# Scores of the second batch: two products a head instead of three, with the keys' high and low parts stacked in the rows

## The chip, the cores and the metric

The kernel runs on one core of a Trainium2 chip. The core has five engines that work at the same time and wait for each other by semaphores: TensorE (PE, matrix products, with its weight loads PEld), VectorE (DVE), ScalarE (ACT), GpSimd (POOL) and SyncE (SP, which issues most of the transfers). The metric is the device time of one execution in microseconds. The time of the kernel before is the median of three runs.

## What is computed

Three layers follow each other. The first is attention over 2 batches of 8 heads, 768 positions, 64 values per head, in which a position sees the 96 positions up to itself and the first 8 of the sequence, with a linear bias by distance:

```
scores = (q @ k.T) / sqrt(64) + bias;  scores = where(keep, scores, -1e9)
a = softmax(scores);  attn = a @ v
```

The second layer normalises each of the 1536 tokens by its root mean square and applies a gated MLP (512 to 1536 and back): `(silu(xn @ w_gate) * (xn @ w_val)) @ w_out`. The third routes each token to two of eight experts by noisy logits and adds the two experts' outputs by their weights.

## The kernel before

The positions are cut into 12 tiles of 128 queries: tiles 0 to 5 are the first batch, 6 to 11 the second. A tile `ti` runs through `prep` (PE transposes its keys and queries into PSUM, other engines copy them out), `scores` (for four pairs of heads: products into one PSUM bank per pair, then on DVE, line 428, bias and minimum, on ACT, line 431, the exponential), `turn` (PE transposes the probabilities, line 444), `values` (products with v, lines 489 and 493) and `rms` and `norm` (normalisation, a small power on POOL in line 574, transposition to xT). The columns of a score product are a window: the tile's own 128 keys and behind them the tile before, whose first 32 places hold the sequence's first keys; tile 6, the first of its batch, has 128 columns, tiles 7 to 11 have 256. `same` copies the keys of the tile before into the window on POOL (line 394).

The score of a product of 64 values fills 64 of PE's 128 rows. Tiles 1 to 11 use all 128: the rows of the key tile `kT` hold an even head in rows 0 to 63 and the odd head beside it in rows 64 to 127, and the query tiles `q..e` and `q..o` hold the even or the odd head in its rows and zeros in the others. `qtile` makes these tiles; the zeros are written once per buffer, on POOL (line 341).

Tiles 6 to 11 (`ti >= F32T`) work with a split of each fp32 number into a high part in the fp32r format and a low part, the difference. `kT[0]` holds the keys' high parts and `kT[1]` their low parts, `q0..` the queries' high and `q1..` their low parts. ACT writes the high parts (line 385), DVE the low ones (line 389 for keys, 391 for queries). A head's scores are the sum of three products (lines 422 to 424): high by high, low by high, high by low.

The stage of tiles 3 to 11 is interleaved with the first chunk of the MLP, so far as tokens are ready. A visit (0, t0, 2) takes two token tiles through four hidden blocks: `up` (line 689, products pz), `hidden` (lines 697 to 703, the last step dl on POOL), `down` (line 716, products acc). Meanwhile `conv` takes apart the MLP's weights (lines 629 to 643, on ACT, POOL and DVE). The kernel is written as a program order with a few forced successions (`follow`); from slot 12 on, a scheduler that simulates the engines' times arranges each engine's instructions. An edit in one place therefore moves instructions around it too. After the last slot the attention's memory is closed and given to the pool `late`, in which further weights of the MLP are put.

Of the kernel before, what the change touches and what calls it, by code (L numbers as in the profile page):

```python
# [9 lines left out]
F32 = mybir.dt.float32  # L10
# [9 lines left out]
P = 128  # L20
# [85 lines left out]
def fused(ctx: ExitStack, tc: tile.TileContext, q, k, v, n_global, n_local, w_gate, w_val, w_out,  # L106
          rms_g, w_router, w_noise, noise, w1, w2, out):
    nc = tc.nc
    w_gate, w_val, w_out = (w.bitcast(I32) for w in (w_gate, w_val, w_out))
    B, H, S, D = q.shape  # L110
# [28 lines left out]
    F32T = NB  # L139
# [145 lines left out]
    qz = {}  # L285
# [44 lines left out]
    def qtile(x, m, ti):  # L330

        key = x, m, ti // NB
        if key not in qz:
            one = m == "e"
            full = ti < F32T
            qz[key] = t = at.tile([P, NP, P], F32 if full else F32R, name=f"q{x}{m}{ti}", tag=f"q{x}{m[0]}", bufs=1 if one else 2)
            r = slice(D, P) if one else slice(0, D)
            if full:
                zero = nc.gpsimd.memset(t[r], 0.0)
            else:  # L340
                zero = nc.gpsimd.tensor_scalar(t[r], ident[r].rearrange("p (o d) -> p o d", o=1).broadcast_to([D, NP, P]),
                                               0.0, None, op0=ALU.mult)
            follow(zero.ins, state["pool"])
        return qz[key]

    def prep(ti, wide, hook=None):
# [5 lines left out]
        qn, kn = state.pop(("in", ti))  # L352
        full = ti < F32T
# [8 lines left out]
        else:  # L362
            qb = [[qtile(x, m, ti) for m in ("e", f"o{ti % 2}")] for x in range(1 if full else 2)]
            qT = {(x, h): qb[x][h % 2][:, h // 2, :] for x in range(len(qb)) for h in range(H)}
            qd = [(slice(m * D, (m + 1) * D), qb[0][m], qb[-1][m]) for m in range(2)]
        operands = ((kn, [(slice(0, P), kT[0][:, :, P:], kT[1][:, :, P:])], 1.0), (qn, qd, -(D ** -0.5)))
        p3s = {}
        state["cur", ti] = (W, C0, nblk, kT, qT)
        for step, (cs, src, dst, sc) in enumerate([(slice(0, NP),) + o for o in operands] if ti else
# [11 lines left out]
            for n, (rs, dh, dl) in enumerate(dst):  # L381
                if wide and n:
                    nc.vector.tensor_scalar(dh[rs, cs], p3[rs, cs], sc, None, op0=ALU.mult)
                else:
                    nc.scalar.activation(dh[rs, cs], p3[rs, cs], AF.Copy, scale=sc)
                if full:
                    continue
                if sc == 1.0:
                    nc.vector.tensor_sub(dl, p3, dh.bitcast(F32))
                else:  # L390
                    nc.vector.scalar_tensor_tensor(dl[rs], p3[rs], sc, dh[rs].bitcast(F32), op0=ALU.mult, op1=ALU.subtract)

        def same(dst, src):
# [14 lines left out]
    def scores(u, wide):  # L408
# [9 lines left out]
        for t in range(2):  # L418
            h = pair(ti, pr)[t]
            sl = slice((h % 2) * D, (h % 2 + 1) * D) if ti < HALF else slice(0, P)  # L420
            o = psc[:, t * W:(t + 1) * W]
            prods = ((0, 0), (1, 0), (0, 1)) if ti >= F32T else ((0, 0),)
            for n, (a, c) in enumerate(prods):
                seq(nc.tensor.matmul(o, qT[a, h], kT[c][sl, h // 2, C0:], start=(n == 0), stop=(n == len(prods) - 1)))  # L424
        for t in range(2):
# [652 lines left out]
    n = 0  # L1078
# [212 lines left out]
```

## Time and profile before

| | |
|---|---|
| median of 3 runs | 792.91 us (789.46 to 793.13) |
| profiled execution | 795.31 us, its span 793.6 us |
| mean granted TensorE clock | 0.992 of full |
| busy: PE, DVE, ACT, POOL | 97%, 59%, 45%, 38% of the span |
| instructions on PE | 5044 products, 5044 weight loads |
| scores of the second batch on PE | 91.6 to 197.3 us |

The profile is one execution, and times in it are counted from the span's start. The durations of PE's products overlap, since they are pipelined; what a product takes from the others is read from the distance of the starts. A view by line groups instructions of one line and shape; a view by stretch gives the busy time between two moments; the timeline shows single instructions, with equal neighbours merged, and in brackets how long the engine stood idle before one and who ended that.

### The profile page before, as it was taken

The page shows a single profiled execution, that of the slowest core. Times are in us where ns is not written, and L with a number is a line of the kernel's source. Part 1 is how long each engine was busy: PE and PEld are TensorE (multiplying, and loading weights), DVE is VectorE, ACT ScalarE, POOL GpSimd, SP SyncE. Part 2 cuts the span into 40 slices and gives each one's busy share as a digit, 9 for nine tenths or more (in the row PEclk, how much of TensorE's full clock was granted, in tenths as well). Part 3 has the DMA queues.
Part 4 walks back from the last instruction along what each step waited for, and adds up shares of the span by engine and source line. Part 5 has one row for each costly group of instructions (what it writes and reads, how often), then busy time and mean ns, then how long its engine had stood idle before and what let it go on. Part 6 is the DMA issues. An engine that isn't in the chain of part 4 may idle for free.

```text
span 793.6 us, 13818 instructions
## 1 busy us (share of the span) xinstructions
PE 768.9 (97%) x5044; PEld 693.6 (87%) x5044; DVE 467.0 (59%) x1073; ACT 358.9 (45%) x800; POOL 305.0 (38%) x343
## 2 busy tenths in 40 slices
PE   8999999999999999999999999799999999999993
PEld 5898999999788888889999889688999999999993
DVE  4898887666477887334445577533545454545542
ACT  5776767665444444113332455433333434344440
POOL 3247852241375566001422244531424343434311
PEclk9999999999999999999999999999999999999997
DMA  8464432260233340010116419953544738282011
GB/s 188 101 182 122 117 97 55 54 173 2 80 120 93 108 132 1 1 53 1 28 27 154 140 32 241 321 172 112 172 146 156 212 113 252 71 258 76 34 41 36
DMA packets 116840, 88.78 MB, mean 112 GB/s; under 512 B 49449, under 2 KB 100649, under 8 KB 116768
## 3 DMA queue, kind: packets, MB, share of 16 engines
q1 hardware_dynamic: 107920, 65.43, 29.9%
q0 software_dynamic: 7120, 19.27, 7.3%
q10 hardware_dynamic: 1728, 3.15, 1.4%
q8 instruction: 42, 0.69, 0.4%
q14 instruction: 30, 0.25, 0.1%
HBM read 75.18 MB, written 13.34 MB: 112 GB/s over the span
## 4 chain that ended last, share of the span: by engine, by line
PE 79%; DVE 7%; issue 5%; ACT 3%; DMA 3%; POOL 1%; POOLq 0%; ACTq 0%; SPq 0%; DVEq 0%
PE pz L983 15%; PE pz L689 13%; PE ac L1023 12%; PE acc L716 12%; PE pv L689 5%; PE pg L689 5%; PE ac L1000 4%; PE ps L424 3%; PE po L493 2%; PE pp L444 2%; PE pg L950 1%; PE lg L785 1%; PE pb L1055 1%; DVE s L428 1%; PE pt L380 1%
## 5 line engine op out<-in xcount | busy, mean ns | idle before, releaser
L983 PE MATMUL pz<-gh,sa 128*128 128x256 f32 (+7 forms) x576 | 155.9, 338 | 0.0
L983 PEld LDWEIGHTS pz<-gh,sa 128*128 128x128 f32 x576 | 103.4, 188 | 4.6
L983 PE MATMUL pz<-gl,sa 128*128 128x256 f32 (+7 forms) x288 | 97.0, 337 | 0.0
L716 PE MATMUL acc<-wo,dh 128*128 128x512 f32 x288 | 88.5, 400 | 1.0 <-ACT dh L702 1.0
L1023 PE MATMUL ac<-zh,sb 128*128 128x480 f32 (+4 forms) x320 | 86.2, 363 | 0.0
L990 ACT ACTIVATE zh<-pz 128x256 fp32r<-128x256 f32 (+7 forms) x72 | 35.1, 488 | 107.8 <-PE pz L983 105.5
L991 DVE SCALAR_TENSOR_TENSOR zl<-pz,zh 128x256 fp32r<-128x256 f32 (+7 forms) x72 | 39.8, 553 | 71.8 <-ACT zh L990 71.5
L689 PE MATMUL pz<-xTh,wg 128*128 128x256 f32 x352 | 75.0, 290 | 1.3 <-ACT xTh L593 1.0
L689 PE MATMUL pz<-xTh,wv 128*128 128x256 f32 x352 | 74.2, 288 | 0.0
L671 ACT ACTIVATE sa<-wab 128x512 fp32r<-128x512 f32 x72 | 45.3, 630 | 56.6 <-PE ac L1023 39.7
L689 PEld LDWEIGHTS pz<-xTh,wg 128*128 128x128 f32 x352 | 58.8, 191 | 3.5 <-ACT xTh L593 1.2
L703 POOL TENSOR_TENSOR dl<-u,dh 128x256 fp32r<-128x256 f32 (+1 forms) x38 | 38.4, 1010 | 60.9 <-ACT dh L702 44.2
L1023 PEld LDWEIGHTS ac<-zh,sb 128*128 128x128 f32 x320 | 58.0, 188 | 3.3
L675 DVE TENSOR_TENSOR sa<-wab,sa 128x512 fp32r<-128x512 f32 x51 | 36.3, 713 | 41.6 <-ACT sa L671 41.3
L716 PEld LDWEIGHTS acc<-wo,dh 128*128 128x128 f32 x288 | 51.1, 188 | 9.9 <-ACT dh L702 1.6
L689 PEld LDWEIGHTS pz<-xTh,wv 128*128 128x128 f32 x352 | 58.1, 190 | 0.4
L431 ACT ACTIVATE p<-s,mx 128x256 f32<-128x256 f32 (+1 forms) x96 | 46.2, 483 | 23.2 <-DVE mx L428 21.8
L893 POOL DMA_INDIRECT metad<-meta,si x24 | 23.8, 991 | 84.6 <-DVE si L865 78.5
L983 PEld LDWEIGHTS pz<-gl,sa 128*128 128x128 f32 x288 | 54.1, 188 | 2.3
L940 POOL DMA_INDIRECT xg<-x2d,ic x30 | 29.8, 994 | 67.1 <-PE pg L950 60.1
L1023 PE MATMUL ac<-zl,sb 128*128 128x480 f32 (+4 forms) x160 | 53.0, 357 | 0.0
L675 DVE TENSOR_TENSOR sb<-wab,sb 128x512 fp32r<-128x512 f32 x67 | 47.2, 704 | 9.5 <-ACT sb L671 8.7
(249 smaller groups left out, 1870.7 us busy)
## 6 DMA issues: line engine op xcount, KB each, us to landing
wab<-in_moe_w_dram SPq DMA_DIRECT2D x128, 256.0 KB, 5.0
rg<-in_moe_w_gate_dram SPq DMA_DIRECT2D x12, 512.0 KB, 3.8
rv<-in_moe_w_val_dram SPq DMA_DIRECT2D x12, 512.0 KB, 3.9
ro<-in_moe_w_out_dram SPq DMA_DIRECT2D x12, 512.0 KB, 3.7
vn<-in_v_dram SPq DMA_DIRECT2D x12, 256.0 KB, 4.6
out_dram<-zero SPq DMA_DIRECT2D x1, 3072.0 KB, 13.9
x2d<-x ACTq DMA_DIRECT2D x12, 256.0 KB, 5.9
kn<-in_k_dram SPq DMA_DIRECT2D x11, 256.0 KB, 3.0
```

Of the source, the lines that this page charges most:

```text
L431: state["e"] = nc.scalar.activation(p[:, :W], s[:, :W], AF.Exp, scale=-1.0, bias=mx[:, h:h + 1], accum_out=sm[:, h:h + 1]).ins
L671: cp = nc.scalar.activation(wp[:, 0], src, AF.Copy)
L675: (nc.gpsimd if pool else nc.vector).tensor_sub(wp[:, 1], src, wp[:, 0].bitcast(F32))
L689: mm = nc.tensor.matmul(pz, a[:, cs], x[:, tt:tt + nt, c, :], start=(n == 0), stop=(n == 3 * DC - 1))
L703: (nc.gpsimd if ci < len(CHUNKS) - 1 else nc.vector).tensor_sub(dl, u, dh.bitcast(F32))
L716: nc.tensor.matmul(acc[t], a[:, tt], w, start=(f == CHUNKS[ci][0] and n == 0), stop=(end and n == 2))
L940: self.last = nc.gpsimd.indirect_dma_start(out=xg[:m], out_offset=None, in_=x2d[:self.rows], in_offset=bass.IndirectOffsetOnAxis(ap=self.i ...
L983: mm = nc.tensor.matmul(pz[:, :cap], a[:, cs], x[:, c, :cap], start=(k == 0), stop=(k == 3 * DC - 1))
L990: nc.scalar.activation(dh[:, :cap], pz[:, :cap], AF.Relu)
L991: nc.vector.scalar_tensor_tensor(dl[:, :cap], pz[:, :cap], 0.0, dh[:, :cap].bitcast(F32), op0=ALU.max, op1=ALU.subtract)
L1000: mm = nc.tensor.matmul(o, a[:, s * P:s * P + m], w[:, cuts(s)[x]], start=(f == 0 and k == 0), stop=(f == FB2 - 1 and k == 2)).ins
L1023: nc.tensor.matmul(acc[c][:, :cap], w[:, c * P:(c + 1) * P], a[:, :cap], start=(f == 0 and k == 0), stop=(f == FB2 - 1 and k == 2))
```

## The change

For tiles 6 to 11 the split parts lie differently. `kT[0]` now belongs to the even heads and `kT[1]` to the odd ones: an even head's high part in rows 0 to 63 and its low part in rows 64 to 127, an odd head's high part in rows 64 to 127 and its low part in rows 0 to 63. The query's high tile `q0..` holds the high part in both halves, by a copy of 64 rows on DVE, where it had zeros; `q1..` holds the low part in the rows of the keys' high part and zeros as before. A head's scores are then two products: `q0` by `kT` gives high by high and high by low in one sum over 128 rows, and `q1` by `kT` gives low by high. For each tile ACT writes the keys' high part in two instructions of 64 rows, DVE subtracts in two instructions of 64 rows that write the other half of the rows, and DVE makes the two copies of the queries' high parts. The zero filling of the three `q0` buffers is gone.

```diff
--- before.py
+++ after.py
@@ -337,6 +337,8 @@
             r = slice(D, P) if one else slice(0, D)
             if full:
                 zero = nc.gpsimd.memset(t[r], 0.0)
+            elif x == 0:
+                return qz[key]
             else:
                 zero = nc.gpsimd.tensor_scalar(t[r], ident[r].rearrange("p (o d) -> p o d", o=1).broadcast_to([D, NP, P]),
                                                0.0, None, op0=ALU.mult)
@@ -363,7 +365,11 @@
             qb = [[qtile(x, m, ti) for m in ("e", f"o{ti % 2}")] for x in range(1 if full else 2)]
             qT = {(x, h): qb[x][h % 2][:, h // 2, :] for x in range(len(qb)) for h in range(H)}
             qd = [(slice(m * D, (m + 1) * D), qb[0][m], qb[-1][m]) for m in range(2)]
-        operands = ((kn, [(slice(0, P), kT[0][:, :, P:], kT[1][:, :, P:])], 1.0), (qn, qd, -(D ** -0.5)))
+        both = [slice(m * D, (m + 1) * D) for m in range(2)]
+        kd = [(both[m], kT[m][:, :, P:], kT[m][:, :, P:]) for m in range(2)]
+        if full:
+            kd = [(slice(0, P), kT[0][:, :, P:], None)]
+        operands = ((kn, kd, 1.0), (qn, qd, -(D ** -0.5)))
         p3s = {}
         state["cur", ti] = (W, C0, nblk, kT, qT)
         for step, (cs, src, dst, sc) in enumerate([(slice(0, NP),) + o for o in operands] if ti else
@@ -386,8 +392,9 @@
                 if full:
                     continue
                 if sc == 1.0:
-                    nc.vector.tensor_sub(dl, p3, dh.bitcast(F32))
+                    nc.vector.tensor_sub(dl[both[1 - n]], p3[rs], dh[rs].bitcast(F32))
                 else:
+                    nc.vector.tensor_copy(dh[both[1 - n]], dh[rs].bitcast(F32))
                     nc.vector.scalar_tensor_tensor(dl[rs], p3[rs], sc, dh[rs].bitcast(F32), op0=ALU.mult, op1=ALU.subtract)
 
         def same(dst, src):
@@ -419,7 +426,7 @@
             h = pair(ti, pr)[t]
             sl = slice((h % 2) * D, (h % 2 + 1) * D) if ti < HALF else slice(0, P)
             o = psc[:, t * W:(t + 1) * W]
-            prods = ((0, 0), (1, 0), (0, 1)) if ti >= F32T else ((0, 0),)
+            prods = ((0, h % 2), (1, h % 2)) if ti >= F32T else ((0, 0),)
             for n, (a, c) in enumerate(prods):
                 seq(nc.tensor.matmul(o, qT[a, h], kT[c][sl, h // 2, C0:], start=(n == 0), stop=(n == len(prods) - 1)))
         for t in range(2):
```

The order of the instructions, engine by engine, in the two built kernels (the numbers behind the names tell tiles and buffers apart; `ps7_0` are the scores of tile 7, first pair; the lines of the changed kernel lie 2 to 7 higher):

PE, the first pair of tile 7 (`kT7` keys, `q0e` and `q1e` the queries' high and low parts), the first head's products and then the second's, before:

```order
L424 MATMUL ps7_0_1510<-kT7_0_1279,q0e6_1070 128x256
L424 MATMUL ps7_0_1510<-kT7_0_1279,q1e6_1074 128x256
L424 MATMUL ps7_0_1510<-kT7_1_1280,q0e6_1070 128x256
L424 MATMUL ps7_0_1510<-kT7_0_1279,q0e6_1070 128x256
L424 MATMUL ps7_0_1510<-kT7_0_1279,q1e6_1074 128x256
L424 MATMUL ps7_0_1510<-kT7_1_1280,q0e6_1070 128x256
```

and now:

```order
L431 MATMUL ps7_0_1507<-kT7_0_1277,q0e6_1070 128x256
L431 MATMUL ps7_0_1507<-kT7_0_1277,q1e6_1072 128x256
L431 MATMUL ps7_0_1507<-kT7_0_1277,q0e6_1070 128x256
L431 MATMUL ps7_0_1507<-kT7_0_1277,q1e6_1072 128x256
```

The two products with `kT7_1`, the third of each head, are gone.

DVE, the preparation of tile 8 (`kT8` keys, `q0e`, `q1e`, `q0o`, `q1o` queries; line 428 the scores' reduction for tile 7, line 501 the output of tile 6), before:

```order
L389 TENSOR_TENSOR kT8_1_1579<-pt8_1580,kT8_0_1578 128x4x128
L501 TENSOR_TENSOR x6_1613<-po6_1370,rs6_1610 128x512
L391 SCALAR_TENSOR_TENSOR q1e6_1074<-pt8_1587,q0e6_1070 64x512
L428 ISA s7_1_1651,mx7_1508<-nbias_74,ps7_2_1644 128x256
L428 ISA mx7_1508 128x1
L428 ISA s7_3_1655,mx7_1508<-nbias_74,ps7_2_1644 128x256
L428 ISA mx7_1508 128x1
L572 TENSOR_SCALAR ss6_1616<-ss6_1616 128x1
L391 SCALAR_TENSOR_TENSOR q1o06_1076<-pt8_1587,q0o06_1072 64x512
```

and now (the lines 428, 501, 389 and 391 are 435, 508, 395 and 398; `CAST` is the copy):

```order
L508 TENSOR_TENSOR x6_1610<-po6_1369,rs6_1607 128x512
L395 TENSOR_TENSOR kT8_0_1571<-pt8_1573,kT8_0_1571 64x4x128
L435 ISA s7_1_1646,mx7_1505<-nbias_74,ps7_2_1641 128x256
L435 ISA mx7_1505 128x1
L397 CAST q0e6_1070<-q0e6_1070 64x512
L398 SCALAR_TENSOR_TENSOR q1e6_1072<-pt8_1582,q0e6_1070 64x512
L435 ISA s7_3_1650,mx7_1505<-nbias_74,ps7_2_1641 128x256
L435 ISA mx7_1505 128x1
L579 TENSOR_SCALAR ss6_1613<-ss6_1613 128x1
L395 TENSOR_TENSOR kT8_1_1572<-pt8_1573,kT8_1_1572 64x4x128
L397 CAST q0o06_1071<-q0o06_1071 64x512
L398 SCALAR_TENSOR_TENSOR q1o06_1074<-pt8_1582,q0o06_1071 64x512
```

Three instructions stood there for tile 8, and now six, with the same reductions between them.

PE, around the end of the value products of tile 11 (`po11`); `pz8_3` are the MLP's products of the last hidden block of the visit before the last in this chunk, `acc0_8` its down products. Before:

```order
L493 MATMUL po11_2865<-rn11_2327,ph11_3_2974 128x64
L689 MATMUL pz8_3_3293<-xTh2_2305,wg3_990 128x256 x2
L689 MATMUL pz8_3_3293<-xTl2_2306,wg3_990 128x256
L689 MATMUL pz8_3_3293<-xTh2_2305,wg3_990 128x256 x2
L689 MATMUL pz8_3_3293<-xTl2_2306,wg3_990 128x256
L689 MATMUL pz8_3_3293<-xTh2_2305,wg3_990 128x256
L689 MATMUL pz8_3_3293<-xTh2_2305,wv3_1159 128x256
L689 MATMUL pz8_3_3293<-xTl2_2306,wv3_1159 128x256
```

and now:

```order
L500 MATMUL po11_2840<-rn11_2314,ph11_3_2947 128x64
L696 MATMUL pz8_3_3266<-xTl2_2293,wv3_1161 128x256
L696 MATMUL pz8_3_3266<-xTh2_2292,wv3_1161 128x256 x2
L696 MATMUL pz8_3_3266<-xTl2_2293,wv3_1161 128x256
L696 MATMUL pz8_3_3266<-xTh2_2292,wv3_1161 128x256 x2
L696 MATMUL pz8_3_3266<-xTl2_2293,wv3_1161 128x256
L696 MATMUL pz8_3_3266<-xTh2_2292,wv3_1161 128x256
L723 MATMUL acc0_8_3197<-wo2_721,dh8_2_3245 128x512 x2
```

Behind the last value product stood 19 products of `pz8_3`, and now 8; the others are ahead of it. Then the same 12 down products follow in both.

## Rows read from the trace of the kernel before

**Rows 1.** the page's part 1: busy time, share of the span, instructions

```profile
PE 768.9 (97%) x5044; PEld 693.6 (87%) x5044; DVE 467.0 (59%) x1073; ACT 358.9 (45%) x800; POOL 305.0 (38%) x343
```

**Rows 2.** by stretch: us, busy PE, PEld, DVE, ACT, POOL; clock, DMA share, GB/s

```profile
84.00:112.00 28.00, 27.36 (x238) 25.78 (x237) 25.61 (x68) 18.57 (x55) 21.28 (x25) 1.00 0.50 134
112.00:127.00 15.00, 15.00 (x134) 13.70 (x133) 10.38 (x28) 9.63 (x26) 3.69 (x7) 1.00 0.23 59
...
176.00:207.00 31.00, 31.00 (x348) 28.91 (x346) 17.41 (x50) 16.48 (x46) 6.30 (x8) 1.00 0.01 2
207.00:216.00 9.00, 7.10 (x51) 5.39 (x48) 3.13 (x6) 5.06 (x11) 5.29 (x7) 1.00 0.53 175
```

**Rows 3.** waits of PE over the span: us in total, times, longest

```profile
PE ps L424 <- DVE mx L428: 1.1, 2, 0.6
...
PE pz L689 <- ACT xTh L593: 1.0, 1, 1.0
```

**Rows 4.** timeline of all engines around the end of the attention

```profile
206.67 0.73 POOL L703 TENSOR_TENSOR dl<-u,dh 128x256 fp32r<-128x256 f32 x1 [4.47 <-issue]
...
207.18 0.19 PE L493 MATMUL po<-rn,ph 128*128 128x64 bf16 x1
...
207.45 0.63 ACT L642 ACTIVATE wg<-wcg 128x512 fp32r<-128x512 f32 x1 [0.92 <-PE po L493]
...
208.16 1.29 POOL L643 TENSOR_TENSOR wg<-wcg,wg 128x512 fp32r<-128x512 f32 x1 [0.77 <-ACT wg L642]
...
209.72 1.30 POOL L643 TENSOR_TENSOR wv<-wcv,wv 128x512 fp32r<-128x512 f32 x1
...
210.98 0.55 POOL L574 TENSOR_TENSOR ri<-ss,mhalf 128x1 f32<-128x1 f32 x1
...
211.67 1.24 POOL L703 TENSOR_TENSOR dl<-u,dh 128x256 fp32r<-128x256 f32 x1
...
215.13 0.50 PE L689 MATMUL pz<-xTh,wg 128*128 128x256 f32 x2 [1.00 <-ACT xTh L593]
```

**Rows 5.** timeline of PE, a pair of tile 8: start, duration, line, operation

```profile
133.12 0.36 PE L424 MATMUL ps<-kT,q0e 128*128 128x256 f32 x1
133.32 0.29 PE L424 MATMUL ps<-kT,q1e 128*128 128x256 f32 x1
133.44 0.40 PE L424 MATMUL ps<-kT,q0e 128*128 128x256 f32 x2
133.68 0.28 PE L424 MATMUL ps<-kT,q1e 128*128 128x256 f32 x1
133.80 0.28 PE L424 MATMUL ps<-kT,q0e 128*128 128x256 f32 x1
133.92 0.27 PE L380 MATMUL pt<-ident,kn 128*128 128x128 f32 x1
```

**Rows 6.** timeline of PE, a pair of tile 6 (128 key columns)

```profile
97.11 0.39 PE L424 MATMUL ps<-kT,q0o 128*128 128x128 f32 x2
97.34 0.27 PE L424 MATMUL ps<-kT,q1o 128*128 128x128 f32 x1
97.45 0.27 PE L424 MATMUL ps<-kT,q0o 128*128 128x128 f32 x1
```

**Rows 7.** groups by line and shape, 0 to 420 us: count, busy us, mean ns

```profile
L389 DVE TENSOR_TENSOR kT<-pt,kT 128x512 fp32r<-128x512 f32 x6 | 4.1, 678 | 1.3 <-ACT kT L385 1.3
L391 DVE SCALAR_TENSOR_TENSOR q1e<-pt,q0e 64x512 fp32r<-64x512 f32 x6 | 4.1, 676 | 0.0
...
L385 ACT ACTIVATE q0e<-pt 64x512 fp32r<-64x512 f32 x6 | 3.5, 584 | 2.2 <-PE pt L380 2.2
...
L462 DVE TENSOR_SCALAR vn<-vn 32x512 int32<-32x512 int32 x8 | 3.4, 429 | 1.6 <-PE po L493 1.6
```

**Rows 8.** line 341 on POOL: count, ns least/median/most, first and last start

```profile
L341 POOL TENSOR_SCALAR q0o<-ident x2: 1490/1711/1932, 72.0 to 90.7; 64x512 fp32r<-64x512 f32 x2
...
L341 POOL TENSOR_SCALAR q0e<-ident x1: 1541/1541/1541, 80.8 to 80.8; 64x512 fp32r<-64x512 f32 x1
```


## The prediction

> **What bounds the kernel now.** I read the page first: TensorE is busy 97% of the span, the next engine (VectorE, DVE) 59% [rows 1]. Such an average covers stages with different limits, so the second view is the busy time stage by stage [rows 2]. The change touches only the six query tiles of the second batch (tiles 6 to 11), whose scores run between 91 and 197 us, interleaved with the first chunk of the gated MLP. From 112 to 207 us PE is busy all the time; DVE has 10.4 of 15 us (69%) at the start of that and 56% towards its end. Only in 84 to 112 us, where the MLP's weights are still being taken apart on DVE, does DVE come near full: 25.6 of 28 us. Third, the waits of PE over the whole span: inside this stretch one wait is charged to a score product, and the two rows of [rows 3] hold about 2 us in all. So in this stage PE is paced by what is queued on it, and a product taken away is time, as long as the next thing on PE is ready.
>
> The one place where it is not is the end of the stage, the fourth view [rows 4]. The last value product of tile 11 ends at 207.2 us. Only then is the memory of the attention free for the next MLP weights: ACT's copy of wg starts at 207.45, POOL makes the low part at 208.16, then wv's at 209.72, then the small power for the norm of tile 11 at 210.98, and only behind these three in its queue the low part dl of the last hidden block, at 211.67. PE needs dl for its last down products, and the norm behind them for the next visit; its first product of that visit starts at 215.13. I call the end of the value products T: T + 7.9 us is set by this chain, not by what PE has left to do. In 207 to 216 PE is busy 7.1 of 9 us.
>
> **The change part by part.** *Removed products.* One of three per head, for 6 tiles of 8 heads: 48 instructions, each with its weight load. What one costs on the queue is the distance between starts, not its duration (which overlaps the next). The six products of a pair of heads start at 133.12, 133.32, 133.44, (133.56), 133.68 and 133.80, and the next instruction at 133.92: 0.20 for the first and 0.12 for each of the others [rows 5]. Tile 6 has only 128 key columns, and its products stand 0.11 apart [rows 6]. The removed one is never the first, so the sum is 40 x 0.12 + 8 x 0.11 = 5.7 us off PE.
>
> That 128 columns cost nearly what 256 do says that these products go at the pace of something other than the columns. The Trainium skill, "TensorE: Matmul & The Clock Gate", section "Back-to-back issue gap", gives N / 2.4 + 2.5 ns at the full clock: an estimate of 56 ns for 128 and 109 ns for 256 columns. The wide rows nearly agree with it (0.12 us), the narrow ones (0.11 us) don't; by it the sum would be 4.8 us instead of 5.7.
>
> *Moved products.* The order is made by a scheduler, and the attention now stands later against the MLP. Counted in the two built orders up to the last value product of tile 11: 461 MLP products of line 689 before, 472 now (all other MLP and attention work is equal), so T has 11 x 0.12 = 1.3 us more in front of it. Behind T there are then 8 of them instead of 19, and they don't matter, since T + 7.9 is set by ACT and POOL, whose order behind T is the same row for row. Also counted: the places where PE comes to an fp32r product from transposes or from value products. They pay the 0.08 us by which the first start in [rows 5] is longer; 103 before, 93 now, so 0.8 us less.
>
> *Added on DVE.* The subtraction for the keys' low part is now two of 64 rows instead of one of 128. Half the rows cost the same: 0.68 us for 64 x 512 as for 128 x 512 [rows 7], so 0.68 us more per tile. No row shows one that writes other rows than it reads; I take the same time. And two copies of 64 x 512 within SBUF. The trace has none; the nearest is the copy of 32 x 512 words, 0.43 us [rows 7], the upper end a subtraction (0.68), the lower nothing. I take 0.43, because its operands lie in SBUF and its length is the same. Per tile 0.68 + 0.86 = 1.54 us (0.68 to 2.04), for six 9.2 us. Cover: a tile takes some 16 us, and DVE stands idle 4.6 of 15 us [rows 2]. Behind a DVE instruction that waits stand the reductions of the scores (line 428), which free the score bank for PE's next pair; between the preparation of a tile and its first product lie three slots of other tiles' work. If that cover were gone, the 9.2 us would be on the path (a rival, below). I count 0.
>
> *Added on ACT.* One more copy of 64 rows per tile, 0.58 us by [rows 7], 3.5 us in all; ACT is busy 53 to 64% there. I count 0.
>
> *Removed on POOL.* Three fillings with zero: 1.54 + 1.49 + 1.93 us [rows 8], all before 93 us, where POOL has 21 of 28 us and makes the low parts of the weights that the MLP waits for. It offsets what DVE gets more there. I count 0, at best the 1 us that PE waits for DVE in [rows 3]. On SP's queue two loads change places with their neighbours; nothing waits for them within 10 us. 0.
>
> **The sum**: -5.7 + 1.3 - 0.8 = -5.2 us at T, and all that follows is the same chain and then a PE that is the bound. The profiled execution took 795.31 us (its span 793.6), so 790.1; it lies 2.4 us above the median of the three runs, and on that median the forecast is 792.91 - 5.2 = **787.7 us**. Its own bounds: 4.4 without the gain at the changes of kind, 6.5 if nothing is lost at T.
>
> **The rivals.**
> A. *DVE's backlog at tiles 6 and 7.* For: in 84 to 112 us DVE has 2.4 us of slack in 28, and two preparations add 2 x 1.54 = 3.1. PE's one wait there is for DVE. Against: the work that PE gets in front (MLP products on finished tokens) needs no new result of DVE, POOL is relieved, and the weights' conversions now stand ahead of the softmax. Price 3.1: a gain of 2.1, 790.8 us on the median.
> B. *DVE sets the pace in all six tiles*: every one of its added instructions delays a reduction of scores, and PE waits for the bank. Price 9.2 - 5.2 = 4.0 us **slower**, 796.9. It decides from the point where DVE is full: against it, 69% plus 1.54 of 15 us makes about 80%.
> C. *The copies hold up POOL.* POOL's low part dl takes 0.73 us alone (206.67) and 1.24 us where a DVE instruction with two SBUF operands runs (211.67) [rows 4], and PE waits for dl. If each of the 12 copies held POOL, and through it PE, by its 0.43 us, 5.2 us would be lost and the gain with it: 792.9. Against: POOL is idle three quarters of the time from 112 us on [rows 2], and dl is needed one block later. The Trainium skill, "SBUF — State Buffer", section "SBUF: two separate sides", calls the port that VectorE and GpSimd share an exclusive lock, held for the whole instruction by a VectorE operation in a two-port mode; the two durations of dl agree with that, and it speaks against this change.
> D. *It doesn't do what it says*: PE is busy by its modelled durations but paced by its producers, so the hole left by a product is filled by waiting. Gain 0 to 1, about 792.4. Against: starts 0.12 us apart without a wait.
>
> **How the numbers follow.** The forecast with its bounds 0.60; a gain above 6.5 (the early waits vanish too) 0.05; A 0.22; C 0.04; D 0.04; B 0.05. A measurement of this kernel can tell about 0.5%, 4.0 us, from no change. Of the forecast's 0.60 some 0.06 lies under 4.0. So faster 0.54 + 0.05 = 0.59; same 0.06 + 0.22 + 0.08 = 0.36; slower 0.05. The range goes from a gain of 6.5 to that of A, 2.1 (786.4 to 790.8), which holds 0.82, and 1.5 us further at each end, since the three runs shown lie 3.7 us apart: 784.9 to 792.3.
>
> **What would show it.** Right: starts of a pair's four products 0.12 apart; T some 5 us earlier, near 202; from T to the next visit's first product again about 7.9 us, with PE idle there by over 1 us more; DVE near 80% without new waits of PE. A: waits of PE for DVE of 1 us and more before 115 us. B: such waits in every tile. C: dl rows of over 1 us and PE waiting for POOL. Wrong altogether: T where it was, at 207.

## The result, and the profile after

The changed kernel takes 798.17 us (796.46 to 803.35, median of 11 runs) against 792.91 before in the same comparison: **slower by 0.7%**, ratio 1.007 with a 95% interval of 1.0053 to 1.0087. Forecast was 787.7. The profiled run took 796.46 us (span 794.7); it began with luck, for the clock rose 8 us earlier than in the run before and the preparation of tile 5 starts at 60.9 us instead of 64.2. From there to the end it is 4.4 us longer than the run before.

The page's first part, to be held against [rows 1]:

```profile
PE 765.0 (96%) x4996; PEld 688.2 (87%) x4996; DVE 478.6 (60%) x1091; ACT 362.5 (46%) x806; POOL 302.0 (38%) x340
```

The 48 products are gone, and VectorE (DVE) has 11.6 us more. By stretch, in the columns of [rows 2]; the first, third and fifth are stretches of it, the second and fourth lie inside:

```profile
112.00:127.00 15.00, 15.00 (x138) 13.81 (x137) 9.70 (x23) 9.22 (x24) 4.43 (x8) 1.00 0.16 37
140.00:150.00 10.00, 7.55 (x77) 6.03 (x75) 9.77 (x27) 7.54 (x20) 5.65 (x7) 1.00 0.35 79
176.00:207.00 31.00, 28.24 (x315) 25.77 (x314) 22.08 (x61) 19.28 (x52) 5.83 (x8) 0.94 0.09 23
180.00:190.00 10.00, 7.35 (x76) 6.35 (x73) 8.22 (x27) 6.63 (x19) 2.75 (x3) 0.83 0.10 23
207.00:216.00 9.00, 7.55 (x61) 5.82 (x59) 2.90 (x5) 3.31 (x8) 4.51 (x6) 1.00 0.54 177
```

PE was busy without a gap from 112 to 207 us in the kernel before, through the preparation of tile 9 too (there in 136 to 146 us, with DVE busy 7.13 of 10) and behind it:

```profile
140.00:150.00 10.00, 10.00 (x108) 9.61 (x105) 5.98 (x19) 6.54 (x20) 3.48 (x7) 1.00 0.06 13
```

Now 2.45 us are missing in 140 to 150, where tile 9 is prepared and DVE is busy 9.77 of 10, and 2.65 in 180 to 190, where tile 11 is. The waits of PE over the span, as [rows 3]; the first stood at 1.1 us before, the second at 0.3, and the third is new:

```profile
PE ps L431 <- DVE mx L435: 3.7, 4, 1.5
...
PE pz L696 <- DVE u L706: 1.7, 2, 1.4
...
PE pp L451 <- DVE kT L395: 1.5, 2, 1.1
```

How such a wait comes about can be read row by row at tile 9. First PE, then DVE (start, duration, line, operation; in brackets the idle time ahead and who ended it):

```profile
142.95 0.39 PE L431 MATMUL ps<-kT,q0o 128*128 128x256 f32 x1 [0.47 <-DVE mx L435]
143.17 0.28 PE L431 MATMUL ps<-kT,q1o 128*128 128x256 f32 x1
143.29 0.28 PE L431 MATMUL ps<-kT,q0o 128*128 128x256 f32 x1
143.41 0.28 PE L431 MATMUL ps<-kT,q1o 128*128 128x256 f32 x1
...
147.32 0.39 PE L431 MATMUL ps<-kT,q0e 128*128 128x256 f32 x1 [1.55 <-DVE mx L435]
...
143.32 0.69 DVE L395 TENSOR_TENSOR kT<-pt,kT 64x512 fp32r<-64x512 f32 x1
144.04 0.84 DVE L397 CAST q0e<-q0e 64x512 fp32r<-64x512 f32 x1
144.92 0.68 DVE L398 SCALAR_TENSOR_TENSOR q1e<-pt,q0e 64x512 fp32r<-64x512 f32 x1
145.53 1.06 DVE L582 SCALAR_TENSOR_TENSOR x<-x,ri,grow 128x512 f32<-128x512 f32 x1
146.51 0.40 DVE L435 CUSTOM_DVE_ANT_0 s<-nbias,ps 128x256 f32<-128x256 bf16 x1
```

PE's four products of a pair start 0.22 us (the first to the second) and 0.12 us apart, near the forecast. The scores of that pair are ready at 143.7, but their reduction (line 435) starts at 146.51: ahead of it in DVE's order stand a key subtraction, a query copy, a query subtraction and a normalisation. PE's next pair needs the bank, and PE, which takes its instructions in order too, stands still for 1.55 us. At tile 7 the wait comes by another way: ahead of a step of the MLP's hidden layer (line 706) stand a query copy of 1.09 us and a query subtraction, and PE's up products wait for that step:

```profile
107.36 0.39 PE L696 MATMUL pz<-xTh,wg 128*128 128x256 f32 x1 [1.38 <-DVE u L706]
```

The new instructions on DVE, grouped (count, busy us, mean ns), 60 to 210 us, against [rows 7]:

```profile
L395 DVE TENSOR_TENSOR kT<-pt,kT 64x512 fp32r<-64x512 f32 x12 | 8.3, 689 | 1.8 <-ACT kT L391 1.5
L398 DVE SCALAR_TENSOR_TENSOR q1o<-pt,q0o 64x512 fp32r<-64x512 f32 x6 | 4.2, 695 | 0.1
...
L397 DVE CAST q0o<-q0o 64x512 fp32r<-64x512 f32 x6 | 3.7, 610 | 0.2
L397 DVE CAST q0e<-q0e 64x512 fp32r<-64x512 f32 x6 | 3.0, 492 | 0.2
```

So the sizes were right: 0.69 us for a subtraction that writes other rows than it reads (forecast 0.68), 0.42 for an undisturbed copy (forecast 0.43), 0.49 and 0.61 in the mean. The chain behind T, as [rows 4]:

```profile
209.78 0.63 ACT L649 ACTIVATE wg<-wcg 128x512 fp32r<-128x512 f32 x1 [3.20 <-PE po L500]
...
210.49 1.31 POOL L650 TENSOR_TENSOR wg<-wcg,wg 128x512 fp32r<-128x512 f32 x1 [3.04 <-ACT wg L649]
...
213.80 0.74 POOL L710 TENSOR_TENSOR dl<-u,dh 128x256 fp32r<-128x256 f32 x1
...
216.76 0.50 PE L696 MATMUL pz<-xTh,wg 128*128 128x256 f32 x2 [0.96 <-ACT xTh L600]
```

T is 209.6, and the next visit starts 7.2 us later. The chain is as forecast, and T itself, the end of the value products, is where it went wrong.

Last, the clock. Behind the waits at tile 11 (PE busy 2.03 of 3.5 us at full clock) the granted clock is 0.51 for 3.5 us, which is its lower level, and then full again:

```profile
182.00:185.50 3.50, 2.03 (x14) 1.57 (x15) 3.42 (x11) 2.60 (x9) 2.33 (x3) 1.00 0.00 0
185.50:189.00 3.50, 3.50 (x37) 3.31 (x36) 1.86 (x9) 2.17 (x6) 0.00 (x0) 0.51 0.02 5
189.00:192.00 3.00, 3.00 (x39) 3.00 (x36) 1.47 (x6) 1.94 (x6) 0.00 (x0) 1.00 0.01 3
```

That costs another 1.7 us. Two sums are used from here on. **Lost** is PE's idle time between 60 and 225 us plus the time lost to the clock (stretch by (1 - granted clock)), both from views of 5 us: before 3.5 + 0, after 10.1 + 1.7. **Query preparation** is, for each of the six tiles, the time from the first query transposition to the end of the last engine's write to its query tiles (the zero fills left out), summed: before 27.7 us, after 43.0. Both sums are of the one profiled execution of a kernel, which lies up to 5.4 us (f2) from the median of its runs.

The 4.4 us from tile 5 to the end come nearly out of these sums: 8.3 more are lost, the products give 5.3 (next section), and the granted clock of the changed kernel falls once more, at 499.6 us, which costs 1.7; that is 4.7.

### The profile page after: what moved, and what is told of

It reads as the page before. It is cut to its first block, busy times and chain, and to the rows that moved or that the text cites. A ratio compares the mean times of both kernels' runs of the same rounds, so it can differ in the third digit from the quotient of the medians.

```text
span 794.7 us, 13741 instructions
## 1 busy us (share of the span) xinstructions
PE 765.0 (96%) x4996; PEld 688.2 (87%) x4996; DVE 478.6 (60%) x1091; ACT 362.5 (46%) x806; POOL 302.0 (38%) x340
## 4 chain that ended last, share of the span: by engine, by line
PE 78%; DVE 9%; issue 6%; DMA 2%; ACT 2%; POOL 1%; SPq 1%; POOLq 0%; ACTq 0%; DVEq 0%
PE pz L990 15%; PE pz L696 13%; PE ac L1030 12%; PE acc L723 11%; PE pv L696 5%; PE pg L696 5%; PE ac L1007 4%; PE ps L431 2%; PE pg L957 2%; PE pp L451 2%; PE po L500 1%; PE po L496 1%; DVE s L435 1%; PE lg L792 1%; PE pb L1062 1%
## 5 line engine op out<-in xcount | busy, mean ns | idle before, releaser
L997 ACT ACTIVATE zh<-pz 128x256 fp32r<-128x256 f32 (+7 forms) x72 | 35.1, 488 | 107.8 <-PE pz L990 107.8
L710 POOL TENSOR_TENSOR dl<-u,dh 128x256 fp32r<-128x256 f32 (+1 forms) x38 | 38.2, 1006 | 69.0 <-ACT dh L709 49.7
L682 DVE TENSOR_TENSOR sa<-wab,sa 128x512 fp32r<-128x512 f32 x51 | 36.4, 714 | 41.6 <-ACT sa L678 41.2
L723 PEld LDWEIGHTS acc<-wo,dh 128*128 128x128 f32 x288 | 51.2, 188 | 10.5 <-ACT dh L709 2.2
```

Source lines behind the costliest of these rows:

```text
L682: (nc.gpsimd if pool else nc.vector).tensor_sub(wp[:, 1], src, wp[:, 0].bitcast(F32))
L710: (nc.gpsimd if ci < len(CHUNKS) - 1 else nc.vector).tensor_sub(dl, u, dh.bitcast(F32))
L723: nc.tensor.matmul(acc[t], a[:, tt], w, start=(f == CHUNKS[ci][0] and n == 0), stop=(end and n == 2))
L997: nc.scalar.activation(dh[:, :cap], pz[:, :cap], AF.Relu)
```

## The experiments

Medians; the kernel before ran beside each and gave 792.8 to 794.6. Ratios are to it, with 95% intervals. The theories in the expectations are numbered anew for each group of runs.

| run | us | ratio | lost, us | query preparation, us |
|---|---|---|---|---|
| before | 792.9 | 1 | 3.5 | 27.7 |
| changed kernel | 798.2 | 1.0053 to 1.0087 | 11.8 | 43.0 |
| e1 products only | 789.5 | 0.9930 to 0.9977 | 4.0 | 30.1 |
| e2 preparation only | 796.0 | 1.0006 to 1.0044 | 5.9 | 41.7 |
| e3 no copies | 788.7 | 0.9908 to 0.9957 | 3.2 | 32.2 |
| e4 keys as before | 795.0 | 0.9995 to 1.0028 | 8.0 | 38.7 |
| f1 copy by ScalarE | 793.5 | 0.9985 to 1.0029 | 6.2 | 39.5 |
| f2 copy behind subtraction | 800.5 | 1.0052 to 1.0114 | 11.8 | 40.6 |
| f3 copy by GpSimd | 796.5 | 1.0023 to 1.0078 | 11.8 | 37.6 |
| x1 copies without reader | 803.8 | 1.0086 to 1.0158 | 16.4 | 49.7 |
| x2 zero fills kept | 798.4 | 1.0041 to 1.0087 | 12.3 | 39.2 |
| x3 tiny copies | 792.8 | 0.9969 to 1.0013 | 6.4 | 36.4 |
| x4 copy by transfer | 800.6 | 1.0066 to 1.0124 | 13.2 | 35.1, transfers not counted |
| g10 attention further ahead | 797.6 | 1.0036 to 1.0082 | 11.0 | 42.9 |
| h1 block held to queries | 799.1 | 1.0042 to 1.0081 | 9.8 | 41.5 |
| h2 block held to keys | 799.5 | 1.0049 to 1.0104 | 8.1 | 41.1 |
| hf1 f1 and hold | 797.2 | 1.0000 to 1.0048 | 10.1 | 42.2 |
| hx4 x4 and hold | 801.6 | 1.0044 to 1.0102 | 12.2 | 32.8, transfers not counted |
| r1 other work off VectorE | 801.9 | 1.0088 to 1.0166 | 12.6 | 41.7 |
| r2 both off VectorE | 795.8 | 1.0005 to 1.0059 | 12.3 | 40.1 |

The fourth column is read first. Taken from the time of the same execution, it leaves 783 to 790 us in the rows with two products (mean 787), whose executions took 787 to 807, and 792 in the two with three: most of the difference between kernels is PE standing still, or running at half clock, in these 165 us.

### The two halves of the change, one at a time

```diff
 e1, from before
-            prods = ((0, 0), (1, 0), (0, 1)) if ti >= F32T else ((0, 0),)
+            prods = ((0, 0), (1, 0)) if ti >= F32T else ((0, 0),)
 e2, from the changed kernel
-            prods = ((0, h % 2), (1, h % 2)) if ti >= F32T else ((0, 0),)
+            prods = ((0, h % 2), (1, h % 2), (0, h % 2)) if ti >= F32T else ((0, 0),)
```

> The preparation of the kernel before, with only two of the three products a head (the high query by the low keys is left out, so the scores are coarser); 48 products fewer and nothing added. Theory 1 (the products are worth what the trace of before says, and the loss comes from the preparation): 5 to 6 us off the kernel before, near 787.5. Theory 2 (the products were never worth that, since the engine then waits for something else): within 1.5 us of the kernel before, 791.5 to 794. Theory 3 (the order in which the scheduler puts things once the products are gone does the harm): slower than before, as the changed kernel is, 796 to 800.

> The preparation of the changed kernel (split key subtractions, query copies, no zero fill), but three products a head again: the third repeats the first, so the scores are wrong and PE has the load that it had before. Theory 1: the preparation costs some 10 us whatever the number of products, so 802 to 804, 5 us over the changed kernel. Theory 2 (products worth nothing): equal to the changed kernel, 797 to 799. Theory 3 (the order is at fault, the preparation is free): near the kernel before, 792 to 795.

e1 gains 3.5 us, between theories 1 and 2. Worked out from the starts of PE's rows between the keys of tile 5 and the last value product, the time from a score product to the next start adds up to 22.9 us before and 17.6 in e1: the 48 products are worth **5.3 us** on the queue (forecast 5.7). The whole stretch is 2.9 us shorter; 0.6 went to five more MLP products, and 2.0 to waits behind down and value products.

e2 costs 3.0 us by the medians (2.0 by the ratio), not 10. And the two don't add up: -3.5 and +3.0 would give 792.4, and the changed kernel has 798.2. Seen another way, taking 48 products out of e2, with the same work on all other engines, makes the kernel 2.2 us **slower**. The reading is that with the new preparation PE is not what sets the time there, and what is taken from it becomes idle time (4.2 us idle in e2, 10.1 in the changed kernel). The order differs between the two as well (267 products of the MLP's first chunk ahead of the keys of tile 9 in e2, 287 in the changed kernel), and no run has the one without the other.

### Which part of the preparation

```diff
 e3, from the changed kernel
-            elif x == 0:
-                return qz[key]
-                    nc.vector.tensor_copy(dh[both[1 - n]], dh[rs].bitcast(F32))
 e4, from the changed kernel
-        if full:
-            kd = [(slice(0, P), kT[0][:, :, P:], None)]
+        kd = [(slice(0, P), kT[0][:, :, P:], kT[-1][:, :, P:])]
-                    nc.vector.tensor_sub(dl[both[1 - n]], p3[rs], dh[rs].bitcast(F32))
+                    nc.vector.tensor_sub(dl, p3, dh.bitcast(F32))
```

> The changed kernel without the twelve copies of the high query; the other half of those tiles is zero filled as before, so the term high query by low keys is left out of the scores. VectorE has 5 us less to do and each query bank is released some 0.8 us earlier. Theory 1a (the copies are the harm): 788 to 790. Theory 1b (the split of the keys' preparation is the harm): 796 to 798. Both by halves: 792 to 794.

> The changed kernel with the keys prepared as before (one ScalarE copy and one VectorE subtraction over 128 rows instead of two of each over 64), the query copies kept and two products a head; the products then take the wrong half, so the scores are wrong. VectorE has 4.1 us less and ScalarE 3.5 us less to do, and the key bank is held some 2.5 us less. Theory 1a (the copies are the harm): 796 to 798. Theory 1b (the keys' split is the harm): 788 to 790. Both by halves: 792 to 794.

e3 is the answer to "which part": without the twelve copies the kernel takes 788.7 us, as fast as e1, although the keys' preparation is split as in the changed kernel. So the key split, 4.2 us more on DVE and 3.5 on ACT, costs nothing by itself, and **the copies cost 9.5 us**, for 6.7 us of DVE time. With the copies there, undoing the key split gives 3.1 us (e4). The four kernels with two products thus form a square: from e1, the split alone adds -0.8 us (e3), the copies alone 5.5 (e4), and both 8.7 (the changed kernel). So 4.0 of the 9.5 us come only where copies and split stand together. In e3 the preparation of tile 9 fills DVE as much as in the changed kernel, and PE doesn't wait:

```profile
129.00:139.00 10.00, 10.00 (x109) 9.57 (x108) 9.63 (x25) 7.66 (x22) 5.42 (x8) 1.00 0.36 80
```

So a full DVE alone is not the cause.

### What of the copies costs: the bank, the engine, the readers

```diff
 f1, instead of the copy
-                    nc.vector.tensor_copy(dh[both[1 - n]], dh[rs].bitcast(F32))
+                    nc.scalar.activation(dh[both[1 - n]], p3[rs], AF.Copy, scale=sc)
 f2: the copy behind the scalar_tensor_tensor instead of ahead of it
 f3, instead of the copy
+                    state["pool"] = nc.gpsimd.tensor_copy(dh[both[1 - n]], dh[rs].bitcast(F32)).ins
 x4, instead of the copy
+                    nc.scalar.dma_start(dh[both[1 - n]].bitcast(F32), dh[rs].bitcast(F32))
 x1, added to e3
+                    nc.vector.tensor_copy(dl[rs], dh[rs].bitcast(F32))
 x3, added to e3
+                    nc.vector.tensor_copy(dh[both[1 - n], 0, :8], dh[rs, 0, :8].bitcast(F32))
 x2, from the changed kernel: the lines "elif x == 0: return qz[key]" left out
```

> The changed kernel, but the second half of the high query is written by ScalarE straight from the transposition's bank, with the scale, instead of by VectorE from the first half. VectorE has 12 instructions and 5 us less to do, ScalarE 12 and some 7 us more (0.58 us each), and the query bank is still read by one more instruction for each half, so it is held as long as in the changed kernel. Theory 1 (VectorE's time is what the copies cost): 788 to 790. Theory 2 (the cost is that the query's bank is held longer, so the next user of the two banks starts late): 796 to 799.

> The changed kernel with the two query instructions on VectorE written in the other order: the subtraction, which reads the bank, first, and the copy, which reads SBUF alone, behind it. The same work, the bank released some 0.4 to 1.1 us earlier a half. Theory 1 (VectorE's time): 797 to 799, as the changed kernel. Theory 2 (the bank): 788 to 791, as without the copies. Between the two, 792 to 795, if each has half.

> The changed kernel with the twelve query copies on GpSimd instead of VectorE, where they take some 1.0 us each by the longer key copies there (12 us more on an engine that is busy 302 of 795 us). VectorE has 5 us less and the bank is released earlier. Theories 1 and 2 both: 788 to 791. Theory 3 (the copies are late wherever they stand, since the scores wait for them, or GpSimd and VectorE slow each other): 794 or more.

f2 gains nothing: the transposition bank, held 0.4 to 1.1 us longer for each half, is not the cause. f1 gains 4.6 us and f3 1.6, and the interval of f3 overlaps that of the changed kernel: half of the loss or less hangs on the copy being on VectorE, and neither is near the 788 to 790 that theory 1 wanted. The copy is not free on any engine. ScalarE takes 0.59 us for it, GpSimd 0.61 at best and 0.77 in the mean (f1, then f3):

```profile
L397 ACT ACTIVATE q0o<-pt 64x512 fp32r<-64x512 f32 x6 | 3.6, 595 | 0.1
```

```profile
L397 POOL CAST q0e<-q0e 64x512 fp32r<-64x512 f32 x6 | 4.6, 775 | 1.7 <-ACT q0e L391 1.4
```

> The kernel without useful copies (e3_no_copies, zero fills kept, the term high query by low keys left out), with twelve copies of the same size put back at the same place on VectorE: each writes the query's low rows, which the subtraction behind it overwrites. So VectorE has the work of the changed kernel again, in the same order and ahead of the same subtraction, and the high tile is ready as early as without copies. Theory 1 (VectorE's time in its full stretches): 796 to 799. Theory 2 (the scores wait for the second half of the high tile, or the scheduler, which knows that they would, orders them later): 788 to 790.

> The kernel without useful copies (e3_no_copies, most of the term high query by low keys left out) with twelve tiny copies, of 64 rows by 8 columns: the high tile now waits for VectorE as in the changed kernel, but the copy is short (the shortest VectorE rows of 64 rows are near 0.1 us, so 1 to 2 us in all instead of 5 to 7). Theory 1 (VectorE's time): 788.5 to 790.5. Theory 2 (readiness and order): 796 to 799.

> The changed kernel with the three zero fills of the high tiles on GpSimd left in, though the copies overwrite what they write: 5 us more on GpSimd before 95 us and nothing else. Theories 1 and 2: 797 to 800, as the changed kernel. Theory 4 (it is the missing zero fills that let the scheduler put the queries' preparation of tile 6 earlier, and with it everything behind): 789 to 792.

> The changed kernel with the twelve copies made by transfers within SBUF (128 KB each, issued by ScalarE right behind its own copy) instead of by VectorE: no engine has the work, but the high tile is complete only when the transfer has landed, some 2 us after its issue. Theory 1 (VectorE's time): 788 to 790, faster than the kernel before. Theory 2 (readiness): no better than the changed kernel, 797 to 801.

x1 is one of the two slowest kernels of all: copies that nobody reads cost 15 us over e3. Theory 2, that it is the scores' waiting for the second half of the high tile, fell with it; those copies do stand ahead of the subtraction that makes the low tile. Tile 11 is where most is lost; the clock falls to 0.59 behind it:

```profile
180.00:190.00 10.00, 7.07 (x76) 5.94 (x75) 9.06 (x25) 7.29 (x20) 3.77 (x4) 1.00 0.52 141
190.00:197.00 7.00, 6.40 (x46) 5.88 (x47) 5.33 (x16) 3.74 (x11) 0.00 (x0) 0.59 0.01 2
```

x3 costs 4.1 us over e3, though its copies move 8 columns. They are not as short as expected either (the rows near 0.1 us that the traces had were of 128 x 1 numbers, none of 64 rows):

```profile
L395 DVE CAST q0o<-q0o 64x8 fp32r<-64x8 f32 x6 | 2.2, 373 | 0.2
L395 DVE CAST q0e<-q0e 64x8 fp32r<-64x8 f32 x6 | 1.2, 200 | 0.2
```

3.4 us for twelve; why is told in the last section. x2 shows that the missing zero fills play no part. x4 was to free every engine and lost all the same: it is no better than the changed kernel, and by the intervals not worse. Its transfers land 3.0 and 3.6 us after their issue (median), and so the high tile is complete later than with any engine's copy:

```profile
q0e<-q0e ACTq DMA_DIRECT2D x6, 128.0 KB, 3.6
q0o<-q0o ACTq DMA_DIRECT2D x6, 128.0 KB, 3.0
```

### The order and the supply of other work

In the built orders 240 and 349 products of the MLP's first chunk stand ahead of the keys of tiles 9 and 11 before, and 287 and 384, which is all that is ready by then, in the changed kernel. That looked like the cause: the work that PE does beside a preparation had been used up.

```diff
 g10
-    LAG = 8
+    LAG = 10
 h1, h2, hf1, hx4: in up(), first product of a block
+                if n == 0 and nm == "g" and hold is not None:
+                    follow(mm.ins, state["pre", hold, False])
```

Here `hold` is tile 9 or 11 for the last block (h2: the third, with the key transpositions) of the visits for tiles 4, 5 and 6, 7, and `state["pre", ...]` the last transposition of that tile's queries (h2: of its keys).

> The changed kernel with one number changed, the lead of attention's slots over the expert visits from 8 to 10 slots: the same instructions in another order. Theory 3 (what the changed kernel lost is an accident of the order, filler used up before the preparations): at least 3 us away from the changed kernel, to either side. Theories 1 and 2: within 2 us of it, 796 to 800.

> The changed kernel with two forced successions on TensorE: the up products of the last hidden block of the visits for tiles 4, 5 and 6, 7 (24 products each, some 2.8 us) stand behind the query transpositions of tiles 9 and 11 instead of ahead of the key transpositions. The same instructions, and 264 and 360 of the MLP's products ahead of tiles 9 and 11 instead of 287 and 384. Theory S (the supply of ready products ran out): the 4.7 and 4.3 us lost at 140 to 150 and 180 to 190 us shrink by 2 to 2.8 each, 793 to 795. Theory C (the chain through VectorE sets the time, and the idle time only shows it): 797 to 799; what is held back is idled away ahead of the preparation instead.

> As the run with the block held to the queries, but it is the third block of those visits that may not start ahead of the key transpositions of tiles 9 and 11, and the fourth, which follows it in its buffers, comes later with it. Theory S: 792 to 795, no worse than the other. Theory C: 797 to 799.

> The kernel whose query copies are made by ScalarE (f1_copy_by_scalare, 793.5), with the same two forced successions as h1_block_held_to_queries; in its order only the one at tile 11 moves something (360 products ahead of it instead of 384). Theory S: its 2.5 us lost at 170 to 190 us go, 790 to 792, better than the kernel before. Theory C: 793 to 795.

> The kernel whose query copies are transfers (x4_copy_by_dma, 800.6), with the same two forced successions (264 and 360 products ahead of tiles 9 and 11 instead of 272 and 384). Theory S: 2 to 4 us better than without, 796.5 to 798.5. Theory C: 800 to 802.

None gains, and hf1 came out slower than either of its theories said. Theory S fell: with the block held back, PE stands still at the same places. In h1:

```profile
140.00:150.00 10.00, 7.94 (x69) 7.04 (x69) 9.18 (x27) 6.19 (x18) 4.98 (x7) 0.91 0.34 78
180.00:190.00 10.00, 8.29 (x88) 7.38 (x84) 8.24 (x24) 7.40 (x21) 2.88 (x3) 1.00 0.04 9
```

g10, h1 and h2, three other orders of the same instructions, lie within 1.4 us of the changed kernel. And x2 has 230 and 364 of those products ahead of tiles 9 and 11, near the 240 and 349 of the kernel before, and is as slow as the changed kernel. A used-up supply is what one sees beside a late attention, not what makes it late.

### Other work off VectorE

```diff
 r1 from the changed kernel, r2 from f1
-            nc.vector.tensor_scalar(a[:32].bitcast(I32), b[:32].bitcast(I32), 0, None, op0=ALU.bitwise_or)
+            nc.gpsimd.tensor_copy(a[:32].bitcast(I32), b[:32].bitcast(I32))
```

> The changed kernel with another small work moved from VectorE to GpSimd: the carrying over of the values' first 32 rows, two instructions of 32 x 512 words a tile (0.42 us each, 10 of them and 4.7 us between 60 and 220 us, as much as the query copies take). The copies stay. Theory C (VectorE's queue in the preparations' stretches sets the time): 3 to 9 us better than the changed kernel, 789 to 795, with under 7 us of PE's idle time and clock loss in 60 to 225 us instead of 11.8. Against it (the loss belongs to the copies' own place in the chain, or to GpSimd, which now gets more): 797 to 801.

> The kernel whose query copies are made by ScalarE (f1_copy_by_scalare, 793.5), with the values' first rows carried over by GpSimd as in r1_other_work_off_vectore: VectorE then has some 9.7 us less than in the changed kernel and about what it has in the kernel before. Theory C: 788 to 791, better than both kernels. Against it: 793 to 796.

Both are slower than the kernels that they came from, by 3.8 and 2.3 us; r2's interval overlaps that of f1. Theory C in its plain form, that any microsecond off VectorE's queue comes back, fell. Why they are slower is not shown: the moved instruction takes longer where it now stands (0.42 us on DVE at the least), and GpSimd comes to it only behind value products, but no wait of another engine is put down to it:

```profile
L469 POOL COPY vn<-vn 32x512 int32<-32x512 int32 x6 | 3.6, 601 | 17.4 <-PE po L500 17.3
...
L469 POOL COPY rn<-rn 32x512 int32<-32x512 int32 x4 | 2.4, 604 | 0.0
```

### What the runs leave standing

In r1, f1, f3 and x4 work is taken off VectorE and put into the same path of a tile elsewhere, longer than it was; each stays 5 to 13 us above e3. The last column of the table fits that for the runs that differ in the copies alone: e3 32.2 us and 788.7; x3 36.4 and 792.8; f1 39.5 and 793.5; changed 43.0 and 798.2; x1 49.7 and 803.8. Each microsecond by which the queries' preparation got longer came with about 0.9 on the time of the whole kernel (15.1 us for 17.5). e1, f2, f3, x2, h1, h2 and r1 lie 2 to 5 us above that line; part of this is that the medians are not of the profiled execution, with whose own time the 16 kernels of two products without transfers lie within 4 us of one line of 0.9 us for each. This is a reading and not shown: the preparation also gets longer because other things are late, and the scheduler arranges each of these kernels anew, so that no run lengthened the preparation while all else stood still. **Settled** is that the copies make the loss, 5.5 us of it alone and the rest together with the keys' split, that 4.9 us of it or more stay when they are made elsewhere, that it is paid in PE's idle time and clock at the preparations, and that neither the bank, the zero fills, a lead of 8 or 10 slots, nor the supply of MLP products is the reason. **Open** is why the scheduled stretch answers 6.7 us of copies with 9.5 us, and in x1 7.9 with 15, 5.6 us more than in the changed kernel for copies at the same place.

No kernel with all three terms beat the one before; e1 and e3 are faster by 0.5 and 0.7%, but leave out the term high query by low keys.

## Why the prediction was wrong, step by step

- **The removed products.** Right in mechanism, near in size: 5.3 us instead of 5.7. The rate that the prediction cites beside its rows (the Trainium skill, "TensorE: Matmul & The Clock Gate", section "Back-to-back issue gap"; 4.8 us by it) is that section's figure for a product by itself, not for a stream in which each product has a weight load, as here. But not all of the 5.3 us reaches T: in e1 and e3, without copies, the way from the keys of tile 5 to T is 2.9 and 3.2 us shorter than before, not 5.2, since waits elsewhere take a part back.
- **Moved products.** Right in number (11 ahead of T), small.
- **Added on DVE, sizes.** Right: 0.69 and 0.42. By the means, 4.2 + 6.7 = 10.9 us instead of 9.2.
- **"I count 0."** This is the step that failed, at the copies: they cost 9.5 us, 5.5 of them without the keys' split. For the keys' split the same 0 held where no copies stand beside it (e3). Of the 10.5 us between the forecast and the measured time these are 9.5; the other 1.0 is what e3, the change without them, falls short of the forecast gain (4.2 instead of 5.2). The prediction compared DVE's busy time with a tile's 15 us and found 20% free. But a tile's DVE work is not spread: within 10 us of a preparation DVE was to be busy 9.8 of 10, and even that cost nothing in e3. What was left out is the path of one tile, transposition, high part, copy, low part, scores, reduction, on engines that take their work in order; that this path is what makes the price is the reading of the section above, not shown. The prediction itself named the reductions queued behind (line 428) and then let the mean decide.
- **The cover was the work removed.** e2 and the changed kernel differ by 48 products, and the one with fewer is slower (796.0 and 798.2): by the reading above, the 5.3 us and the copies' cover were the same PE time. The forecast took both.
- **ACT and POOL at 0.** Held, ACT's copies in e3 and POOL's missing zero fills in x2.
- **Behind T** 7.9 us were forecast and 7.2 came; e1 and e3 have about 7 too.
- **Rivals.** B gave the nearest time (796.9), but its mechanism, every added DVE instruction at full price in all tiles, is not what happened: the key split was free without the copies, the longest waits came at tiles 7, 9 and 11, and copies off DVE still cost 4.9 us and more. A's sign came once (1.38 us at 107.36), but the waits go on after 115 us. C's sharing is real (below), but PE waits for dl no longer than 0.2 us. D is refuted by e1.
- **The chances.** Slower had 0.05, because the only way there was to pay every added microsecond in full. That a price can be more than the work itself was no case at all.

## What to carry to other kernels

An engine that is busy 69% need not have 31% free for an instruction that stands between two stages of the same tile: ask where in the tile's path it stands and what is queued behind it at that moment, not how full the engine is on average. Standing in the path does not settle the price either: the keys' split stands there too and was free without the copies. When the engine that bounds a stage gets less work, the time that hid the others' work may go with it; give a change that trades work between engines a real chance of being slower. A change of two parts is best priced one part at a time, and then both together, for here the halves gave -3.5 and +3.0 us and the whole +5.3.

## What the hardware showed that was not expected

**A tiny copy can take as long as its neighbour on GpSimd.** In x3 a copy of 64 x 8 words takes 0.17 us in eight of twelve cases, and 0.97 where GpSimd has a two-operand instruction running (DVE, then POOL):

```profile
179.66 0.97 DVE L395 CAST q0o<-q0o 64x8 fp32r<-64x8 f32 x1
```

```profile
179.56 1.04 POOL L326 TENSOR_TENSOR rn<-vn 128x512 f32<-128x512 f32 x1 [4.25 <-DVE mx L433]
```

The copy ends at 180.63, when GpSimd's instruction ends (180.60): it was held for as long as that ran. The three other long ones (0.22, 0.33 and 0.60 us) end 0.02 to 0.03 us behind a GpSimd instruction that started before them, too; a GpSimd instruction on 128 x 1 numbers, which ran from 159.88 to 160.43, did not hold the copy at 160.15 (0.17 us). In the changed kernel the 64 x 512 copy takes 0.42 us undisturbed and 1.09 at 105.05, beside the same line of GpSimd (104.83 to 105.87). The Trainium skill, "SBUF — State Buffer", section "SBUF: two separate sides", calls the port that the two share an exclusive lock, held for the whole instruction by whichever starts first; the rows of the held copies agree. The prediction had looked at the one direction only, GpSimd held up by VectorE. In the changed kernel the copies held longest are at tiles 7, 9 and 11 (1.09, 0.84 and 0.75 us), where PE waits, but that is not the reason of the loss: in f2 all six copies of these tiles take 0.42 to 0.47 us, and PE waits at the same tiles (11.8 us lost).

**Waits can be paid twice.** Behind a stretch of waits the granted clock can drop to its lower level. In the runs of the table the time lost to it in this stage is none, 1.7, 3.4 or 5.1 us; it made 1.7 us of the changed kernel's loss and 5.1 of x1's. The waits at tile 9 in the changed kernel (2.45 us of 10) were not followed by such a fall, those at tile 11 were.

**Two readers of a PSUM bank take turns in this program.** ScalarE's second copy of the keys waits, by a semaphore, for VectorE's first subtraction on the same bank (0.33 us at 141.79); whether the chip would need it, no run shows. The bank of the keys is held 34.1 us in the six tiles instead of 15.8, and that costs nothing in e3 (30.7 us).
